# Sparse attention and a two-layer FFN on one core: block-diagonal query tiles, and an order of work taken from a modelled timeline

## Chip, cores, metric

The kernel runs on one core of a Trainium2 chip. The metric is device time in microseconds (us), lower is better. The engines are named as the profile names them: PE is TensorE (PEld its weight loads), ACT ScalarE, DVE VectorE, POOL GpSimd, SP SyncE. Each takes its instructions in the order in which the program put them in its queue.

## What is computed

```python
B, H, S, D = q.shape                      # 8, 8, 576, 64
scores = scale * np.matmul(q, k.transpose(0, 1, 3, 2))
mask_local = (rel >= 0) & (rel < stride)  # stride 32, heads 0 to 3
mask_strided = (rel >= 0) & (pos[None, :] % stride == pos[:, None] % stride)  # heads 4 to 7
...                                       # masked softmax
attn_out = np.matmul(attn, v)
x = attn_out.transpose(0, 2, 1, 3).reshape(B * S, H * D)   # 4608 x 512
r = np.maximum(x @ w_in, 0.0)             # 512 x 2048
out = (s * (r * r) + b) @ w_out           # 2048 x 512
```

## The kernel before

Attention runs batch by batch, four pairs of heads in each: pairs 0 and 1 are local, 2 and 3 strided. A local pair cuts the 576 positions into six blocks of 96 queries with 128 keys; a strided one into eight groups of 72. `pair_steps(b, m)` lists the steps of a pair: transposes of q and k into `ps_t` (L169), copied to `qTl`, `kT_loc`, `qTs`, `kTs` by ScalarE (L180, L185); scores into `ps_s` (L205), one matmul per head and block, on 64 of the 128 rows, since a head has 64 values and a pair of heads (or of groups) lies in the two halves; exp on ScalarE (L211) and a mask product on VectorE (L216) into `pt`; the product with v into `ps_a` (L234), whose last column is the row sum; reciprocal (L240) and division (L242) into `x_nat`; the transposes back (L257) and the copy into `xT` (L263, L265). `load_qk`, `load_v`, `load_w_in` and `load_w_out` are issued by POOL; `pair_heads` has four VectorE copies (L121) that put the two heads of local q and k side by side.

The FFN goes over nine blocks of 512 rows. `ffn_steps(T)` gives 64 matmuls of 512 columns for the first product (`ff1`, L302: 16 groups of four, then relu L307 on ScalarE and the square L308 on VectorE into `gT`) and 64 for the second (`ff2`, L317: four groups of 16, then L322 on VectorE and a store by SP). `emit_bcs` (L340) sums w_out's rows for the bias once.

Of the eight banks of PSUM `ps_t` and `ps_s` have two each, `ps_a` one, `ps_f` three. The order is the program's own (`manual_schedule`). Batch 0 runs alone; then block T of the FFN is emitted with the steps of batch T + 1 spread between its first 112 matmuls at an even distance:

```python
for i, f in enumerate(seq):
    at.setdefault(int(i * 112 / len(seq)), []).append(f)
```

Blocks 7 and 8 have no batch beside them. What ScalarE and VectorE do for a step is emitted with its last matmul, so all queues have the order of the steps.

Of the kernel before, what the change touches and what calls it, by code (L numbers as in the profile page):

```python
# [9 lines left out]
FP16 = mybir.dt.float16  # L10
FP32 = mybir.dt.float32
AF = mybir.ActivationFunctionType
ALU = mybir.AluOpType


@with_exitstack
def kernel(
# [64 lines left out]
    sched = ctx.enter_context(tc.manual_schedule())  # L82

# [11 lines left out]
    for i in range(2):  # L95
        nc.vector.memset(kT_loc[i][:, 0:LPAD], 0.0)

# [50 lines left out]

    def pair_steps(b, m):
# [5 lines left out]
        half = nt // 2  # L155
        nk = 128 if loc else SQ
        st = {}
        T, SS, A0, A1, X = [], [], [], [], []

        def trans(name, j):  # L160
            def f():
                if j == 0:
                    st["p" + name] = psum.tile([128, S], FP16, tag="t", bufs=2, name="ps_t")
                ps = st["p" + name]
# [5 lines left out]
                    out=ps[:, nq * j:nq * j + nq], lhsT=src,  # L170
                    rhs=ident[0:nq, 0:nq], is_transpose=True)
                if j == nt - 1:
                    if loc:
                        if name == "q":
                            st["q"] = qkp.tile([128, S], FP16, tag="qTl", name="qTl")
                            dst = st["q"]
                        else:
                            st["k"] = kT_loc[mm]
                            dst = st["k"][:, LPAD:LPAD + S]
                        nc.scalar.copy(  # L180
                            out=dst.rearrange("d (p j) -> d p j", j=nt),
                            in_=ps.rearrange("d (j p) -> d p j", j=nt))
                    else:
                        st[name] = qkp.tile([128, S], FP16, tag=name + "Ts", name=name + "Ts")
                        nc.scalar.copy(out=st[name], in_=ps)  # L185
            return f

        for name in ("q", "k"):
            for j in range(nt):
                T.append(trans(name, j))  # L190

        def grp(j):

            return (j // half, j % half) if loc else (j % 2, j // 2)

        def score(e, j):
            def f():
                g, i = grp(j)
                if i == 0:
                    st["s", e, g] = psum.tile([128, 3 * LQ], FP32, tag="s", bufs=2, name="ps_s")  # L200
                ps = st["s", e, g]
                c = i * nq
                r0, at = (64 * e, j * nq) if loc else (64 * (j % 2), (4 * e + j // 2) * nq)
                rr = slice(r0, r0 + 64)
                nc.tensor.matmul(  # L205
                    out=ps[0:nk, c:c + nq], lhsT=st["k"][rr, at:at + nk],
                    rhs=st["q"][rr, at:at + nq])
                if i == half - 1:
                    pt = ptp.tile([128, half, nq], FP16, tag="pt" + sfx, name="pt")
                    st["pt", e, g] = pt  # L210
                    nc.scalar.activation(  # L211
                        out=pt[0:nk].rearrange("k t c -> k (t c)"),
                        in_=ps[0:nk, 0:half * nq], func=AF.Exp, scale=scale)
                    mask = (mask_loc if loc else mask_str)[:, None, :].to_broadcast(
                        [nk, half, nq])
                    nc.vector.tensor_tensor(out=pt[0:nk], in0=pt[0:nk], in1=mask, op=ALU.mult)  # L216
            return f

        for a in range(2):
# [185 lines left out]
```

## Time and profile before

| | |
|---|---|
| median of 3 runs (lowest to highest) | 461.65 us (460.33 to 464.23) |
| the profiled execution: time, span | 465.23 us, 463.5 us |
| mean granted TensorE clock | 0.979 |
| busy: PE, DVE, ACT, POOL | 393.1, 198.6, 177.7, 100.1 us |
| matmuls | 2736 |
| HBM read, written | 38.08, 9.44 MB |

A matmul of the profile lasts longer than its slot: matmuls are pipelined, their ends are modelled, and the distance of two starts is what one costs. So busy time says little for TensorE; its timeline and the waits say more. All numbers of the profile belong to the one profiled execution.

### The profile page before, as it was taken

Reading aid. Unit: us, or ns where it says so; the run is one execution under the profiler, and the core shown is the slowest. Engines: PE = TensorE matmul, PEld = TensorE weight load, DVE = VectorE, ACT = ScalarE, POOL = GpSimd, SP = SyncE. Lnnn points to the kernel's source line nnn. Section 1 sums busy time; section 2 is a strip of 40 time slices with the busy share of each in tenths; the row PEclk is TensorE's granted clock in tenths of the full one; section 3 lists DMA queues with packets and bytes.
Section 4 is the critical chain, followed back from the end, with each engine's and each line's share of the span. In section 5 each row is a group of like instructions: output and inputs, shape, how many; then the busy total and the mean of one; then the engine's idle time right before and its main releaser. Section 6 shows DMA issues by size and latency. Waiting matters only on the chain.

```text
span 463.5 us, 6912 instructions
## 1 busy us (share of the span) xinstructions
PE 393.1 (85%) x2736; PEld 194.7 (42%) x2736; DVE 198.6 (43%) x557; ACT 177.7 (38%) x354; POOL 100.1 (22%) x137
## 2 busy tenths in 40 slices
PE   1848799788978989788978898888969797999995
PEld 0633344344434444344434343444434343444442
DVE  1552434444453444434444444434444355352431
ACT  2614651065503751065414651166305541260530
POOL 6736436510244012510252022400000000000000
PEclk9999999899999999899999999899999999899999
DMA  8999999960567114850458025700001001101101
GB/s 108 93 204 100 164 156 141 88 103 1 60 75 87 32 25 60 68 102 0 61 75 119 1 30 67 82 24 1 24 24 45 1 0 47 45 2 46 47 23 69
DMA packets 72516, 28.99 MB, mean 63 GB/s; under 512 B 53028, under 2 KB 67876, under 8 KB 72484
## 3 DMA queue, kind: packets, MB, share of 16 engines
q0 software_dynamic: 66640, 19.04, 44.1%
q1 hardware_dynamic: 5844, 9.51, 5.6%
q8 instruction: 21, 0.34, 0.3%
q14 instruction: 11, 0.09, 0.1%
HBM read 38.08 MB, written 9.44 MB: 103 GB/s over the span
## 4 chain that ended last, share of the span: by engine, by line
PE 71%; DVE 9%; ACT 7%; DMA 6%; issue 3%; POOL 2%; ACTq 0%; POOLq 0%
PE ps_f L302 27%; PE ps_f L317 26%; PE ps_s L205 9%; DVE x_nat L242 5%; PE ps_a L234 4%; ACT u L307 4%; DMA kl<-in_k_dram 3%; PE ps_t L169 3%; DMA qs<-in_q_dram 2%; ACT kT_loc L180 2%; DVE rec L240 2%; PE ps_t L257 1%; DVE o L322 1%; DVE gT L308 1%; ACT kTs L185 1%
## 5 line engine op out<-in xcount | busy, mean ns | idle before, releaser
L302 PE MATMUL ps_f<-xT,w_in_sb 128*128 128x512 f16 x576 | 178.2, 388 | 0.0
L317 PE MATMUL ps_f<-w_out_sb,gT 128*128 128x512 f16 x576 | 166.9, 393 | 0.0
L307 ACT ACTIVATE u<-ps_f 128x512 f16<-128x512 f32 x144 | 86.0, 597 | 72.9 <-PE ps_f L302 72.3
L308 DVE TENSOR_TENSOR gT<-u 128x512 f16<-128x512 f16 x144 | 61.3, 426 | 109.2 <-ACT u L307 109.2
L317 PEld LDWEIGHTS <-gT 128*128 128x128 f16 x576 | 58.0, 102 | 39.1 <-issue 4.3
L234 PEld LDWEIGHTS <-pt 72*72 72x72 f16 (+1 forms) x448 | 44.1, 127 | 71.3 <-DVE x_nat L242 58.3
L211 ACT ACTIVATE pt<-ps_s 72x288 f16<-72x288 f32 (+1 forms) x128 | 48.2, 407 | 59.8 <-PE ps_s L205 58.4
L302 PEld LDWEIGHTS <-w_in_sb 128*128 128x128 f16 x576 | 56.8, 99 | 33.4 <-issue 0.6
L234 PE MATMUL ps_a<-v_str,pt 72*72 72x65 f16 x256 | 39.1, 211 | 29.1 <-DVE x_nat L242 28.8
L265 ACT COPY xT<-ps_t 128x576 f16<-128x576 f16 x16 | 10.2, 639 | 108.6 <-PE ps_t L257 108.6
L242 DVE TENSOR_TENSOR x_nat<-ps_a,rec 72x256 f16<-72x256 f32 (+1 forms) x96 | 44.6, 465 | 3.3
L322 DVE SCALAR_TENSOR_TENSOR o<-ps_f,s_sb,bcs 128x512 f32<-128x512 f32 x36 | 26.9, 747 | 37.1 <-PE ps_f L317 37.1
L134 POOL DMA_DIRECT2D v_str<-in_v_dram x32 | 28.0, 875 | 65.5 <-PE ps_a L234 45.4
L240 DVE RECIPROCAL rec<-ps_a 72x4 f32<-72x4 f32 (+1 forms) x96 | 17.4, 181 | 53.3 <-PE ps_a L234 52.5
L234 PE MATMUL ps_a<-v_loc,pt 128*96 128x65 f16 x192 | 27.3, 209 | 13.2 <-DVE x_nat L242 13.2
L205 PE MATMUL ps_s<-qTl,kT_loc 64*128 64x96 f16 x192 | 26.3, 221 | 11.3 <-ACT kT_loc L180 11.3
L205 PE MATMUL ps_s<-qTs,kTs 64*72 64x72 f16 x256 | 34.4, 222 | 0.8 <-ACT pt L211 0.5
L205 PEld LDWEIGHTS <-kTs 64*72 64x72 f16 x256 | 16.6, 112 | 33.1 <-issue 32.8
L257 PE MATMUL ps_t<-ident,x_nat 72*128 72x72 f16 (+1 forms) x224 | 29.9, 215 | 0.5 <-DVE x_nat L242 0.5
L133 POOL DMA_DIRECT2D v_loc<-in_v_dram x32 | 28.7, 898 | 6.1 <-DVE x_nat L242 2.3
L216 DVE TENSOR_TENSOR pt<-pt,mask_str 72x288 f16<-72x288 f16 x64 | 19.0, 304 | 25.2 <-ACT pt L211 25.1
L205 PEld LDWEIGHTS <-kT_loc 64*128 64x128 f16 x192 | 11.6, 95 | 40.2 <-issue 23.5
(37 smaller groups left out, 251.3 us busy)
## 6 DMA issues: line engine op xcount, KB each, us to landing
out_dram<-o SPq DMA_DIRECT2D x36, 256.0 KB, 2.1
v_loc<-in_v_dram POOLq DMA_DIRECT2D x32, 80.0 KB, 3.5
ql<-in_q_dram POOLq DMA_DIRECT2D x8, 288.0 KB, 5.3
kl<-in_k_dram POOLq DMA_DIRECT2D x8, 288.0 KB, 6.2
qs<-in_q_dram POOLq DMA_DIRECT2D x8, 288.0 KB, 6.6
ks<-in_k_dram POOLq DMA_DIRECT2D x8, 288.0 KB, 8.1
v_str<-in_v_dram POOLq DMA_DIRECT2D x32, 72.0 KB, 3.6
w_in_sb<-in_moe_w_in_dram POOLq DMA_DIRECT2D x4, 512.0 KB, 9.7
```

The lines of the kernel that those rows point to most:

```text
L133: nc.gpsimd.dma_start(out=vl[:, h, 1:LT, 0:D], in_=src)
L134: nc.gpsimd.dma_start(out=vs[:, h, :, 0:D], in_=v[b, 4 + h].rearrange("(p j) d -> p j d", j=ST))
L205: nc.tensor.matmul(out=ps[0:nk, c:c + nq], lhsT=st["k"][rr, at:at + nk], rhs=st["q"][rr, at:at + nq])
L211: nc.scalar.activation(out=pt[0:nk].rearrange("k t c -> k (t c)"), in_=ps[0:nk, 0:half * nq], func=AF.Exp, scale=scale)
L234: nc.tensor.matmul(out=ps[0:nq, j % per, :], lhsT=st["pt", e, grp(j)[0]][0:nk, grp(j)[1], :], rhs=vt[0:nk, 2 * mm + e, j, :])
L242: nc.vector.tensor_tensor(out=st["x"][:, j0:j0 + per, 64 * e:64 * e + 64], in0=ps[0:nq, 0:per, 0:D], in1=rec[0:nq, 0:per].to_broadcast([nq ...
L257: nc.tensor.matmul(out=ps[:, nq * j:nq * j + nq], lhsT=st["x"][:, j, :], rhs=ident[0:nq, 0:nq], is_transpose=True)
L302: nc.tensor.matmul(out=st["h"], lhsT=w_in_sb[:, ct, ft * 128:(ft + 1) * 128], rhs=xT[ct][:, tok0:tok0 + PS], start=(ct == 0), stop=(ct == 3))
L307: nc.scalar.activation(out=u, in_=st["h"], func=AF.Relu)
L308: nc.vector.tensor_tensor(out=st["g"][:, ft, :], in0=u, in1=u, op=ALU.mult)
L317: nc.tensor.matmul(out=st["o"], lhsT=st["g"][:, ft, ts * 128:(ts + 1) * 128], rhs=w_out_sb[:, ft, :], start=(ft == 0), stop=(ft == NFT - 1))
L322: nc.vector.scalar_tensor_tensor(out=o, in0=st["o"], scalar=s_sb[:, 0:1], in1=bcs, op0=ALU.mult, op1=ALU.add)
```

## The change

Three parts:

- A pair's transposed q goes into a tile `qD` in two half copies: head (or group) 0 into columns 0 to nq - 1 of rows 0 to 63, the other into the next nq columns of rows 64 to 127; the rest is zeroed once at the start. One score matmul on all 128 rows then gives both heads (or groups): 28 a batch instead of 56, of 192 or 144 columns. `ps_s` groups hold two (local) or three (strided) of them; exp and mask go over these groups.
- `ps_f` is split: two banks `ps_f1`, one bank `ps_f2`. First and second product each have a list of their own, and the second product of a block can run between groups of the first of the next.
- All steps are emitted by a loop that keeps a modelled time `plan.t`. A step may go when its inputs are done by the model; ScalarE and VectorE work is emitted in the order in which the model has it ready, copies on the engine that would end them earlier. Attention goes first while its share lags behind the FFN's (`due`), and up to three pairs are open. Loads have modelled arrivals: constants at the start, later 12 us (q, k local), 16.5 us (strided) and 16 us (v) after the call, which follows the last k transpose, or the last product with v, of the batch two earlier.

```diff
+class Plan:
...
+    LAT = 70.0
...
+    def flush(self):
+        while True:
+            best = None
+            for p in self.pend:
+                r = self.ready_at(p[0])
+                if r is not None and r <= self.t and (best is None or r < best[0]):
+                    best = (r, p)
+            if best is None:
+                return
+            r, p = best
+            self.pend.remove(p)
+            eng = min(p[1], key=lambda e: max(self.free[e], r) + p[1][e])
+            end = max(self.free[eng], r) + p[1][eng]
+            self.free[eng] = end
+            p[2](eng)
+            for k in p[3]:
+                if isinstance(k, Group):
+                    k = ("rel", k.tag, k.n)
+                self.done[k] = end + self.LAT
...
+    def emit(self, s):
+        if s.group is not None:
+            s.group.n = self.count.get(s.group.tag, 0)
+            self.count[s.group.tag] = s.group.n + 1
+        s.fn()
+        self.t += s.ns
+        for k in s.keys:
+            self.done[k] = self.t + self.LAT + 60
+        for p in s.posts:
+            self.post(*p)
...
+    qD_loc = [const.tile([128, LT, 2, LQ], FP16, name=f"qD_loc{i}") for i in range(2)]
+    qD_str = [const.tile([128, ST, 2, SQ], FP16, name=f"qD_str{i}") for i in range(2)]
...
+        nc.vector.memset(qD_loc[i], 0.0)
+        nc.vector.memset(qD_str[i], 0.0)
...
+    TB, SB, AB, F1B, F2B = 2, 2, 1, 2, 1
+
+    def copy_on(eng, **kw):
+        (nc.scalar.copy if eng == "A" else nc.vector.tensor_copy)(**kw)
...
+                    def half(e):
+                        def g(eng):
+                            hs = slice(64 * e, 64 * e + 64)
+                            ps, qD = st["pq"], st["q"]
+                            if loc:
+                                copy_on(eng,
+                                        out=qD[hs, :, e, :].rearrange("d t (p j) -> d t p j", j=nt),
+                                        in_=ps[hs].rearrange("d (j t p) -> d t p j", j=nt, t=nt))
+                            else:
+                                copy_on(eng, out=qD[hs, :, e, :],
+                                        in_=ps[hs].rearrange("d (j p) -> d j p", j=nt))
+                        return g
+
+                    s.posts = [([key], {"A": 620, "V": 750}, half(e), [("q", e, id_)])
+                               for e in range(2)]
...
-                r0, at = (64 * e, j * nq) if loc else (64 * (j % 2), (4 * e + j // 2) * nq)
-                rr = slice(r0, r0 + 64)
+                if i % per_s == 0:
+                    st["s", g] = psum.tile([128, 3 * 2 * SQ], FP32, tag="s", bufs=SB, name="ps_s")
+                c = i % per_s * 2 * nq
                 nc.tensor.matmul(
-                    out=ps[0:nk, c:c + nq], lhsT=st["k"][rr, at:at + nk],
-                    rhs=st["q"][rr, at:at + nq])
-                if i == half - 1:
-                    pt = ptp.tile([128, half, nq], FP16, tag="pt" + sfx, name="pt")
-                    st["pt", e, g] = pt
+                    out=st["s", g][0:nk, c:c + 2 * nq], lhsT=st["k"][:, i * nq:i * nq + nk],
+                    rhs=st["q"][:, i].rearrange("d e c -> d (e c)"))
...
+                s.posts = [([key], {"A": 170 + 0.83 * 2 * n * nq}, ex, [("e", id_, g), group]),
+                           ([("e", id_, g)], {"V": 150 + 0.52 * 2 * n * nq}, ms,
+                            [("p", id_, g)])]
...
+                s.posts = [([key], {"V": 185}, rc, [("r", id_, e, j)]),
+                           ([("r", id_, e, j)], {"V": 150 + 1.1 * 64 * per}, mu,
+                            [("x", id_, e, j), group])]
...
+            s.posts = [([key], {"A": 600}, rl, [("u", T, ft), group]),
+                       ([("u", T, ft)], {"V": 430}, sq, [("g", T, ft)])]
...
+            s.posts = [([key], {"V": 760}, ev, [group])]
...
+    def fetch(b, at):
+
+        load_qk(b)
+        arrive([("in", "ql0", b), ("in", "kl0", b)], at)
+        arrive([("in", "qs", b), ("in", "ks", b)], at + 4500)
+        plan.post([("in", "ql0", b), ("in", "kl0", b)], {"V": 2000},
+                  lambda eng: pair_heads(b), [("in", "ql", b), ("in", "kl", b)])
+
+    fetch(0, 10000.0)
     load_v(0)
+    arrive([("in", "vl", 0), ("in", "vs", 0)], 22500.0)
     load_w_in()
-    load_qk(1)
+    for c in range(4):
+        arrive([("w_in", c)], 25700.0 + 2700 * c)
+    fetch(1, 38000.0)
     load_v(1)
+    arrive([("in", "vl", 1), ("in", "vs", 1)], 48000.0)
     load_w_out()
-    pair_heads(0)
-    seq, last = batch_steps(0)
-    for f in seq + last:
-        f()
-    pair_heads(1)
+    arrive([("w_out",)], 61000.0)
...
+        if b + 2 < B:
+            def more_qk(b=b):
+                fetch(b + 2, plan.t + 12000.0)
+
+            def more_v(b=b):
+                load_v(b + 2)
+                arrive([("in", "vl", b + 2), ("in", "vs", b + 2)], plan.t + 16000.0)
+            last_t.after = more_qk
+            last_av.after = more_v
...
+        pos = (i1 + i2) / 64.0 + 0.1
+        return (pos if pos <= 1 else 1 + (pos - 1) / 2) * batch_ns
...
+        active = [p for p in range(len(att)) if at_i[p] < len(att[p])][:3]
+        for p in active:
+            r = plan.step_ready(att[p][at_i[p]])
+            if r is not None and r <= plan.t:
+                cand = p
+                break
...
+        order = []
+        if i1 < len(f1):
+            order.append(1)
+        if i2 < len(f2):
+            order.append(2)
+        if len(order) == 2 and i1 % 4 == 0 and i1 > i2 + 64:
+            order.reverse()
+        if i1 % 4:
+            order = [1]
+        for o in order:
+            s = f1[i1] if o == 1 else f2[i2]
+            r = plan.step_ready(s)
+            if r is not None and r <= plan.t:
+                main = o
+                break
+        if cand is not None and (att_done < due() or main is None):
+            s = att[cand][at_i[cand]]
+            plan.emit(s)
+            at_i[cand] += 1
+            att_done += s.ns
+        elif main == 1:
+            plan.emit(f1[i1])
+            i1 += 1
+        elif main == 2:
+            plan.emit(f2[i2])
...
```

## Rows read from the trace of the kernel before

**Rows 1.** The page, part 1: busy us (share of the span) x instructions of each engine.
```profile
PE 393.1 (85%) x2736; PEld 194.7 (42%) x2736; DVE 198.6 (43%) x557; ACT 177.7 (38%) x354; POOL 100.1 (22%) x137
```

**Rows 2.** Chain that ended last, in order of time: start us, length us, what.
```profile
95.67 0.51 issue
...
352.16 0.51 issue
...
403.13 13.81 PE ps_f L302 x64
...
458.42 0.75 DVE o L322
```

**Rows 3.** Timeline of TensorE: start us, us, engine, line, operation, tiles, shapes, count.
```profile
301.09 0.38 PE L302 MATMUL ps_f<-xT,w_in_sb 128*128 128x512 f16 x1
301.31 0.25 PE L169 MATMUL ps_t<-ident,qp 96*128 96x96 f16 x2
301.40 0.38 PE L302 MATMUL ps_f<-xT,w_in_sb 128*128 128x512 f16 x1
...
316.24 0.38 PE L302 MATMUL ps_f<-xT,w_in_sb 128*128 128x512 f16 x1
316.46 0.24 PE L234 MATMUL ps_a<-v_loc,pt 128*96 128x65 f16 x2
316.53 0.38 PE L302 MATMUL ps_f<-xT,w_in_sb 128*128 128x512 f16 x1
```

**Rows 4.** The same timeline where the score matmuls (L205) are interleaved.
```profile
303.58 0.39 PE L302 MATMUL ps_f<-xT,w_in_sb 128*128 128x512 f16 x1
303.90 0.22 PE L205 MATMUL ps_s<-qTl,kT_loc 64*128 64x96 f16 x2
304.05 0.39 PE L302 MATMUL ps_f<-xT,w_in_sb 128*128 128x512 f16 x1
304.37 0.21 PE L205 MATMUL ps_s<-qTl,kT_loc 64*128 64x96 f16 x1
304.52 0.39 PE L302 MATMUL ps_f<-xT,w_in_sb 128*128 128x512 f16 x1
```

**Rows 5.** Waits from 301.62 to 352.16 us: us in total, times, longest.
```profile
PEld L205 <- issue: 7.8, 34, 0.3
...
PE ps_a L234 <- DVE x_nat L242: 5.3, 7, 1.6
...
PE ps_s L205 <- ACT kT_loc L180: 1.4, 2, 0.9
```

**Rows 6.** Timeline of all engines around one wait for x_nat.
```profile
316.99 0.19 PE L234 MATMUL ps_a<-v_loc,pt 128*96 128x65 f16 x1
317.57 0.43 DVE L308 TENSOR_TENSOR gT<-u 128x512 f16<-128x512 f16 x1 [0.70 <-ACT u L307]
...
318.14 0.55 DVE L242 TENSOR_TENSOR x_nat<-ps_a,rec 96x384 f16<-96x384 f32 x1
...
318.75 0.23 PE L234 MATMUL ps_a<-v_loc,pt 128*96 128x65 f16 x1 [1.56 <-DVE x_nat L242]
```

**Rows 7.** Groups of instructions: xcount | busy us, mean ns | idle before.
```profile
L180 ACT COPY qTl<-ps_t 128x576 f16<-128x576 f16 x16 | 10.2, 638 | 17.5 <-PE ps_t L169 17.4
...
L263 DVE COPY xT<-ps_t 128x576 f16<-128x576 f16 x16 | 7.2, 451 | 3.6 <-PE ps_t L257 3.5
```

**Rows 8.** Timeline of POOL: where w_out and the loads of batch 2 are issued.
```profile
45.11 1.18 POOL L145 DMA_DIRECT2D w_out_sb<-in_moe_w_out_dram  x1
...
46.95 0.71 POOL L104 DMA_DIRECT2D kl<-in_k_dram  x1
```

**Rows 9.** The view of tile kl: its eight loads, from issue to landing.
```profile
DMA to landing us min/median/max: 5.7/6.2/17.2
```

**Rows 10.** Timeline of VectorE: the two copies that pair k of batch 1.
```profile
37.38 0.62 DVE L121 COPY kp<-kl 96x768 f16<-96x768 f16 x2 [2.11 <-DMA kl<-in_k_dram]
```

**Rows 11.** Timeline of TensorE in batch 0, where only attention runs.
```profile
29.55 0.45 PE L234 MATMUL ps_a<-v_str,pt 72*72 72x65 f16 x4 [0.72 <-DVE x_nat L242]
```

More of the change, by code (lines that the diff above doesn't have):

```diff
@@ L13, with __init__, ready_at, post @@
 ALU = mybir.AluOpType
+class Plan:
+    LAT = 70.0
+    def __init__(self):
+        self.t = 0.0
+        self.done = {}
+        self.pend = []
+        self.free = {"A": 0.0, "V": 0.0}
+        self.count = {}
+    def ready_at(self, needs):
+        if any(k not in self.done for k in needs):
+            return None
+        return max([self.done[k] for k in needs], default=0.0)
+    def post(self, needs, cost, fn, keys):
+        self.pend.append((needs, cost, fn, keys))
+    def flush(self):
[17 more added lines that the diff above has]
+                self.done[k] = end + self.LAT
+    def step_ready(self, s):
+        r = self.ready_at(s.needs)
+        if r is None:
+            return None
+        if s.group is not None:
+            n = self.count.get(s.group.tag, 0)
+            if n >= s.group.bufs:
+                k = ("rel", s.group.tag, n - s.group.bufs)
+                if k not in self.done:
+                    return None
+                r = max(r, self.done[k])
+        return r
+    def emit(self, s):
+        if s.group is not None:
+            s.group.n = self.count.get(s.group.tag, 0)
[6 more added lines that the diff above has]
+            self.post(*p)
+        if s.after is not None:
+            s.after()
+    def advance(self):
+        nxt = [v for v in self.done.values() if v > self.t]
+        assert nxt, "nothing left that could make a step ready"
+        self.t = min(nxt)
@@ L16, with __init__ @@
+class Group:
+    def __init__(self, tag, bufs):
+        self.tag, self.bufs, self.n = tag, bufs, None
+class Step:
+    def __init__(self, fn, ns, needs=(), group=None, keys=(), posts=(), after=None):
+        self.fn, self.ns, self.needs, self.group = fn, ns, needs, group
+        self.keys, self.posts, self.after = keys, posts, after
 @with_exitstack
@@ L224, in pair_steps, with p_of, av @@
+            return s
+        gr = None
+        for i in range(nt):
+            if i % per_s == 0:
+                gr = Group("s", SB)
+            steps.append(score(i, gr))
+        def p_of(e, j):
+            i, r = (j, e) if loc else (4 * e + j // 2, j % 2)
+            return i // per_s, i % per_s * 2 + r
         per = nt if loc else nt // 2
         vt = (v_loc if loc else v_str)[b % NV]
-        def av(e, j):
+        def av(e, j, group):
             def f():
@@ L253, in f, with xtrans @@
+                s.posts = [([key], {"V": 185}, rc, [("r", id_, e, j)]),
+                           ([("r", id_, e, j)], {"V": 150 + 1.1 * 64 * per}, mu,
+                            [("x", id_, e, j), group])]
+            return s
+        for e in range(2):
+            for j in range(nt):
+                if j % per == 0:
+                    gr = Group("a", AB)
+                steps.append(av(e, j, gr))
+        st["last_av"] = steps[-1]
+        def xtrans(j, group):
             def f():
@@ L342, in emit_bcs, with arrive @@
         nc.scalar.activation(out=bcs, in_=ps, func=AF.Copy, scale=b_sb)
-    load_qk(0)
+    def arrive(keys, at):
+        for k in keys:
+            plan.done[k] = at
+    def fetch(b, at):
[5 more added lines that the diff above has]
+    fetch(0, 10000.0)
@@ L378 @@
+    while plan.pend:
+        plan.flush()
+        if plan.pend:
+            plan.advance()
 _INS = ['q', 'k', 'v', 'moe_w_in', 'moe_w_out', 'moe_s', 'moe_b']
```

295 lines of the change are left out of this document (157 added, 138 removed).

## Prediction, made before the changed kernel ran

> **What bounds the kernel now.** The page's busy shares come first: TensorE 85%, ScalarE and VectorE under half [rows 1]; so TensorE is the engine to look at, and what it stands still for. The chain of waits gives the period. Six times in the middle of the kernel it passes the same point of the loop over blocks, from 95.67 to 352.16 us; that is five periods, (352.16 - 95.67) / 5 = 51.3 us each [rows 2]. The stretch at its end has no attention in it: 64 products take 13.81 us, 215.8 ns each [rows 2]. The 128 products of a block are then worth 128 x 0.2158 = 27.6 us, so seven periods carry 51.3 - 27.6 = 23.7 us each for one batch of attention. The question is what those 23.7 us are.
>
> The timeline of TensorE answers it. Two small matmuls of 96 columns between two large ones stretch the distance of the large ones from 0.216 to 0.31 us, so each costs 0.047; with 65 columns, 0.29 us, so 0.037 [rows 3]. The 56 transposes of q and k, 56 products with v and 28 transposes back of a batch cost 140 x about 0.04 = 5.6 us. The score matmuls, which use 64 rows of the array, behave differently: the distance is 0.47 us, with two of them in it and with one [rows 4]. So 0.47 - 0.216 = 0.25 us is paid per interruption, of which the columns explain about 0.04 to 0.08; the remaining 0.17 to 0.21 us goes into changing between 64 and 128 rows. The table of waits counts 34 of these in one period [rows 5]; 34 x 0.25 = 8.5 us, of which about 6.5 us is changing over.
>
> The rest, 23.7 - 5.6 - 8.5 = 9.6 us, is standing still. The table of waits names two [rows 5]: TensorE waits 7 times for the normalised x_nat (5.3 us), twice for kT_loc (1.4 us). These waits count from the modelled end of the matmul before, 0.38 - 0.216 = 0.16 us after its issue slot, so nine waits are worth 9 x 0.16 = 1.5 us more: 8.2 of the 9.6 us are found. The longest shows why [rows 6]: ps_a has one buffer; the last product before it starts at 316.99, but VectorE first does a square (gT, which itself waited for the relu) and only then the division that frees ps_a, and TensorE starts at 318.75. It is an order problem, not a full engine.
>
> **The change, part by part.**
>
> *Block-diagonal queries.* Per batch 56 score matmuls of 64 rows become 28 of 128 rows: 12 with 192 columns and 16 with 144. 512 columns in 0.2158 us are 2.37 columns per ns, and 96 columns cost 0.047; with 0.004 to spare for each they take 12 x 0.085 + 16 x 0.065 = 2.1 us. That replaces 8.5 us: 6.4 us saved per batch. The Trainium skill speaks against this step: "TensorEngine Tiling (Array Packing)", section Theoretical Speedup, gives products with 64 contraction rows up to twice the rate when they are packed in row tiles. The trace agrees that a packed second score matmul is free (0.47 us with one or two). By that rule alone the step would lose half of the new 2.1 us, 1.1 us a batch; by the rows the interruption outweighs it.
> The price outside TensorE is that a q copy becomes two half copies, each of 64 partitions and still 576 long. On ScalarE one costs what a whole copy costs, 0.638 us [rows 7]. On VectorE no row shows the regrouping copy; the plain one from PSUM takes 0.451 [rows 7], and twice that, 0.9, is my upper bound. I take 0.75, which is nearer to ScalarE's row. Four more copies a batch are 2.6 us, in a period in an engine pair that is busy for 38 and 43% [rows 1]: hidden. If the cover goes, it is 2.6 x 8 = 21 us at most. Zeroing the four qD tiles stands on VectorE before the first load has landed, and costs nothing. The exponentials and masks get fewer and longer, the same elements: nothing.
>
> *Order from the plan, second product beside the first.* Steps are put in TensorE's queue when the plan takes their inputs for ready, and the work of ScalarE and VectorE in the order in which it becomes ready. A square whose relu isn't done no longer stands before a division, and with second-product matmuls as filler there is nearly always something to issue. I expect the 9.6 us per period to fall, not to vanish: the queues stay in order, and the plan gives 0.13 us from the end of a matmul's slot to its reader, where the rows give 0.16 us of pipeline and a start a few hundredths later. With some 36 bank groups a batch and 0.03 to 0.04 us late at each, that is 1.3 us. Bounds: 0 and 9.6.
> Cost at the end: ps_f2 has one bank, and the last three groups of the second product have nothing beside them. Each waits for an eviction of 0.75 us [rows 2] and two hand-overs, about 1.0 us: 3 us.
>
> *The start, which gets worse.* The diff gives every later load a fixed arrival, 12 us after the plan's time of the call. For batch 2 this is wrong. I followed the plan by hand from its own constants, for the order alone: products with v of batch 0 are held until 22.5, the last k transpose of batch 0 comes at about 26.4, so pair_heads(2) counts as ready at 38.4, directly behind pair_heads(1) at 38.0 and ahead of all but the first square of block 0 and all masks of batch 1. On the chip POOL issues these loads only behind w_out, which goes out at 45.11; kl follows at 46.95 [rows 8] behind it. The longest of the eight loads of kl took 17.2 us [rows 9]; I take it for this one, so it lands at 64.15. POOL's order up to there is not changed. VectorE finishes pair_heads(1) at 38.0 [rows 10] and then stands in pair_heads(2) until 64.15 + 0.62 = 64.8 us. Behind it: u has three buffers, so ScalarE stops at the fifth relu, ps_f1 has two banks, so TensorE stops after some six groups. From about 40 to 64.8 nearly nothing moves.
>
> *The sum.* At 64.8 the work still to do before the dense part is 10 groups of first product and batch 1. Its limit is the single ps_a bank: the four products (0.45) and the wait for their division (0.72) took 1.17 us per group [rows 11], and for six I take 1.4. Twelve groups are 8 x 1.17 + 4 x 1.4 = 15.0 us, behind about 6 us of transposes, scores, exponentials and masks: 85.8 us. Then on TensorE 1152 - 64 = 1088 products x 0.2158 = 234.8; the 16 bias products 3.5 and the wait for their copy, as long as that of an eviction, 1.0; six batches x (5.6 + 2.1 = 7.7) = 46.2; six x 1.3 = 7.8 of stalls; 3 at the end; and 463.5 - 458.4 = 5.1 from the last product to the end of the span [rows 2]. 85.8 + 234.8 + 4.5 + 46.2 + 7.8 + 3 + 5.1 = 387.2 us of span. The profiled execution took 465.23 for a span of 463.5, so 389 us; the median of the runs, 461.65, is 0.8% under it: **386 us**. Both ends of the unknowns: stalls 0 gives 378, a slow VectorE copy with no cover adds up to 21.
>
> **Rivals.**
> *A: as above*, 376 to 401.
> *B: the early stall doesn't arise* (pair_heads(2) falls later in VectorE's queue than I put it, or the loads land earlier). For it: my order is worked out by hand. Against it: it needs the plan's ready time to move from 38 to over 60 us. The dense part would begin at about 61 us, where the diff itself puts the landing of w_out, 24.8 us earlier: 386 - 25 = 361.
> *C: the drains go but the standing still stays.* For it: the queues are in order, ps_a still has one bank, and nothing in the trace has run this order. Against it: VectorE and ScalarE are busy for under half, and the waits found are order waits. With 9.6 us left per period instead of 1.3 the time is 386 + 6 x 8.3 = 436; half of it, 411.
> *D: slower than before.* One mechanism: at each of the 36 bank groups of a batch TensorE arrives at the moment the plan names and the operand is late, with nothing allowed past. The waits for x_nat now cost 5.3 / 7 + 0.16 = 0.92 us each. If each group cost that, 36 x 0.92 x 6 = 199 us would come on top. It decides from (462 - 378) / 216 = 0.39 us a group. Against it: scores and products with v have other pairs and FFN steps between them, so their inputs mostly wait for them.
>
> **How the numbers follow.** A 0.58, B 0.14, C 0.20, D 0.08. The likeliest is A, 386 us. The range must hold 0.8: from 361, which keeps most of B, to 420, which holds the lower half of C; outside are D (0.08), the upper part of C (0.08) and the lower edge of B (0.03). A change under about 1% cannot be told from none with this kernel's runs; A, B and C all lie beyond 1% on the fast side. Faster 0.92, within 1% 0.02, slower 0.06.
>
> **What would show it.** In the changed kernel: no wait of the score weights with "issue" as its releaser, and 28 score matmuls a batch; VectorE idle from about 38 to 64 us with the releaser DMA kl at a pairing copy; large products every 0.216 us once attention is done; a mean of under 38 us per batch in the middle. I would be wrong if that idle stretch is missing or shorter than 15 us (B), or if waits for x_nat, pt or copies still sum to over 5 us per batch (C).

## The result, and the profile after

The changed kernel takes **408.0 us** (median of four runs, 406.4 to 409.1) against 461.0 for the kernel before on the same chip: a ratio of 0.884, with a 95% interval of 0.878 to 0.890. The forecast was 386 us: the change is faster as forecast, by 22 us less. The profiled execution took 407.57 us, 405.5 of them span; the sum had given 387.2 us of span.

The page of the changed kernel: part 1 (busy us, share of the span, instructions), and of part 2 the rows of TensorE and of its granted clock, in 40 slices of 10.1 us.

```profile
PE 338.8 (84%) x2512; PEld 187.8 (46%) x2512; DVE 198.0 (49%) x545; ACT 183.9 (45%) x338; POOL 101.5 (25%) x137
...
PE   0665505967999799979997999799899999999884
...
PEclk9999955985999999989999999999999999999999
```

Against [rows 1] TensorE has 224 matmuls fewer and is still busy for the same share. The row in slices says where to look: a 5 and a 0 in the slices from 41 to 61 us, a 6 and a 7 from 81 to 101 us, and from there one weaker digit in every fourth slice, which is once per batch. From 295 us on it is full but for the end. The clock has its 5s in and right behind the two weak stretches, and one 8 in the slice from 172 to 182 us.

The chain of waits: start us, length us, what.

```profile
46.21 17.34 DMA kl<-in_k_dram
...
67.45 1.71 PE ps_f L448 x4
...
97.71 5.51 PE ps_f L506 x16
...
103.98 1.02 PE ps_f L484 x4
...
141.87 0.86 PE ps_f L484 x4
...
180.05 1.42 PE ps_f L484 x4
...
258.08 0.86 PE ps_f L484 x4
...
400.88 0.75 DVE o L495
```

It passes the same point, the first groups of a block, at 141.87 and three periods later at 258.08: 116.21 / 3 = 38.7 us a batch, where [rows 2] gave 51.3. Its last piece, from 400.88, is the copy behind the last product. It also shows the start: a load of `kl` that lasts until 63.6, and then no bias (L506) before 97.7. The sum had put that at 85.8.

The clock is in both of these means. In the changed kernel two of the three periods took 38.2 us; the one from 180.05 to 219.91 took 39.9, and it begins with four large matmuls in 1.42 us instead of 0.86, at a granted clock of 0.50 from 180.5 to 183.5. In the kernel before, three of the five periods took 51.7 to 52.0 us at a mean granted clock of 0.97, and two took 50.5 at 1.00. The second of these two is the period whose waits [rows 5] counts, here in the windows view (the last section names its columns):

```profile
301.62:352.16 50.54, 43.79 (x326) 21.68 (x325) 23.30 (x67) 20.74 (x43) 0.00 (x0) 1.00 0.06 22
```

At the full clock a period thus fell from 50.5 to 38.2 us.

The early stall is where the working by hand had put it. The timeline of VectorE (start us, us, engine, line, operation, tiles, shapes, idle before and its releaser):

```profile
37.91 0.62 DVE L217 COPY kp<-kl 96x768 f16<-96x768 f16 x2
62.10 0.62 DVE L217 COPY qp<-ql 96x768 f16<-96x768 f16 x2 [23.57 <-DMA ql<-in_q_dram]
63.57 0.62 DVE L217 COPY kp<-kl 96x768 f16<-96x768 f16 x2 [0.84 <-DMA kl<-in_k_dram]
64.11 1.56 DVE L467 TENSOR_TENSOR gT<-u 128x512 f16<-128x512 f16 x4
```

The pairing copies of batch 2 stand in VectorE's queue directly behind those of batch 1 [rows 10], and for 23.6 us nothing behind them runs. Three squares stood there ready, one for each buffer of `u`; the fourth relu waited for the first of them, and first products stood behind that.

The table of waits over the whole execution (us in total, times, longest us), with the rows that answer to [rows 5] and one of the stall:

```profile
ACT u L463 <- DVE gT L467: 19.5, 1, 19.5
...
PE ps_a L373 <- DVE x_nat L391: 8.4, 14, 1.3
...
PE ps_t L269 <- ACT qD_loc L248: 7.6, 4, 1.9
...
PEld L324 <- issue: 2.7, 9, 0.5
```

The score weights' wait for "issue", 34 times and 7.8 us in the one period of [rows 5], is down to 9 times and 2.7 us in the whole execution. The wait for `x_nat`, 7 times and 5.3 us a period there, is down to 14 times and 8.4 us in all. The relu's 19.5 us for the squares is the stall as ScalarE saw it. What else is new is a wait of up to 1.9 us for a copy into `qD_loc`.

### The profile page after: what moved, and what is told of

The parts are those of the page before. It is cut to its first block, busy times and chain, and to the rows that moved or that the text cites. A ratio compares the mean times of both kernels' runs of the same rounds, so it can differ in the third digit from the quotient of the medians.

```text
span 405.5 us, 6425 instructions
## 1 busy us (share of the span) xinstructions
PE 338.8 (84%) x2512; PEld 187.8 (46%) x2512; DVE 198.0 (49%) x545; ACT 183.9 (45%) x338; POOL 101.5 (25%) x137
## 4 chain that ended last, share of the span: by engine, by line
PE 73%; DMA 11%; ACT 5%; DVE 5%; POOL 4%; issue 2%; POOLq 0%; ACTq 0%
PE ps_f L484 30%; PE ps_f L448 29%; DMA kl<-in_k_dram 4%; DMA ks<-in_k_dram 4%; PE ps_a L373 4%; PE ps_t L269 3%; PE ps_s L324 3%; DMA qs<-in_q_dram 3%; ACT qD_loc L248 2%; PE ps_t L412 2%; DVE qD_loc L248 2%; DVE x_nat L391 1%; PE ps_f L506 1%; ACT pt L337 1%; DVE o L495 1%
## 5 line engine op out<-in xcount | busy, mean ns | idle before, releaser
L448 PE MATMUL ps_f<-xT,w_in_sb 128*128 128x512 f16 x576 | 165.5, 392 | 20.7 <-ACT u L463 19.0
L484 PE MATMUL ps_f<-w_out_sb,gT 128*128 128x512 f16 x576 | 156.2, 381 | 4.4 <-DVE o L495 3.6
L448 PEld LDWEIGHTS <-w_in_sb 128*128 128x128 f16 x576 | 56.0, 100 | 69.2 <-issue 24.6
L337 ACT ACTIVATE pt<-ps_s 128x384 f16<-128x384 f32 (+2 forms) x96 | 44.3, 488 | 18.3 <-PE ps_s L324 18.1
L373 PE MATMUL ps_a<-v_str,pt 72*72 72x65 f16 x256 | 32.8, 207 | 7.3 <-DVE x_nat L391 7.2
L248 ACT COPY xT<-ps_t 128x576 f16<-128x576 f16 x30 | 19.2, 639 | 38.1 <-PE ps_t L412 37.9
L229 POOL DMA_DIRECT2D v_loc<-in_v_dram x32 | 28.6, 894 | 16.5 <-DMA v_loc<-in_v_dram 8.9
L205 POOL DMA_DIRECT2D qs<-in_q_dram x8 | 5.9, 743 | 97.6 <-PE ps_t L269 97.6
L324 PE MATMUL ps_s<-qD_str,kTs 128*72 128x144 f16 x128 | 23.5, 238 | 1.1 <-ACT kTs L248 0.8
L324 PE MATMUL ps_s<-qD_loc,kT_loc 128*128 128x192 f16 x96 | 18.7, 274 | 5.6 <-ACT kT_loc L248 4.3
L373 PE MATMUL ps_a<-v_loc,pt 128*96 128x65 f16 x192 | 21.3, 213 | 1.2 <-DVE x_nat L391 1.2
L412 PEld LDWEIGHTS <-x_nat 72*128 72x128 f16 (+1 forms) x224 | 16.3, 104 | 11.2 <-DVE x_nat L391 6.8
L224 POOL DMA_DIRECT2D v_loc<-in_v_dram x32 | 17.4, 543 | 14.4 <-DMA w_out_sb<-in_moe_w_out_dram 10.4
```

The lines of the kernel that those rows point to most:

```text
L248: (nc.scalar.copy if eng == "A" else nc.vector.tensor_copy)(**kw)
L324: nc.tensor.matmul(out=st["s", g][0:nk, c:c + 2 * nq], lhsT=st["k"][:, i * nq:i * nq + nk], rhs=st["q"][:, i].rearrange("d e c -> d (e c)"))
L337: nc.scalar.activation(out=pt[0:nk, 0:2 * n].rearrange("k t c -> k (t c)"), in_=st["s", g][0:nk, 0:2 * n * nq], func=AF.Exp, scale=scale)
L373: nc.tensor.matmul(out=st["a"][0:nq, j % per, :], lhsT=st["pt", g][0:nk, i, :], rhs=vt[0:nk, 2 * mm + e, j, :])
L412: nc.tensor.matmul(out=st["px"][:, nq * j:nq * j + nq], lhsT=st["x"][:, j, :], rhs=ident[0:nq, 0:nq], is_transpose=True)
L448: nc.tensor.matmul(out=gts["h"], lhsT=w_in_sb[:, ct, ft * 128:(ft + 1) * 128], rhs=xT[ct][:, tok0:tok0 + PS], start=(ct == 0), stop=(ct == 3))
```

## The experiments

Each was timed in three rounds beside the kernel before on the same chip. Ratios are to the kernel before, with 95% intervals. Runs made on different occasions are compared by their ratios, times 461.65 us.

The theory to begin with: the loss is the early stall, and order and tiles do in the middle what the sum says. The rivals: that some of the loss lies in the middle, in the order or in the tiles, or that what holds the start is not the stall.

**1. The true arrival of batch 2's loads.** The changed kernel, with the landing of these loads told to the plan as it was measured:

```diff
-                fetch(b + 2, plan.t + 12000.0)
+                fetch(b + 2, 64000.0 if b == 0 else plan.t + 12000.0)
...
-                arrive([("in", "vl", b + 2), ("in", "vs", b + 2)], plan.t + 16000.0)
+                arrive([("in", "vl", b + 2), ("in", "vs", b + 2)],
+                       73000.0 if b == 0 else plan.t + 16000.0)
```

> The changed kernel with two constants of the plan set to what the trace shows for batch 2: its q and k at 64 us (12 us after the call before), its v at 73 us. Nothing else differs. Theory (VectorE stands in pair_heads(2) and holds everything): VectorE has no idle stretch of over 5 us between 38 and 62 us, block 0's first product and batch 1 run there, and the dense part begins at about 70 us instead of 104; half a batch of attention that ran before 98 us now runs later (4 us): 375 to 386 us against 408. Rival (the machine waits for the loads anyway, so the stall is only the form the wait takes): less than 8 us gained, 400 to 408.

Measured: 394.3 us, 0.850 [0.845, 0.855]. By the ratios that is (0.884 - 0.850) x 461.65 = 16 us faster than the changed kernel, and a miss all the same. VectorE's stall of 23.6 us is gone. The timelines of VectorE, then of TensorE, in this kernel show what took its place:

```profile
74.34 0.62 DVE L217 COPY qp<-ql 96x768 f16<-96x768 f16 x2 [6.71 <-DMA ql<-in_q_dram]
...
76.89 0.39 PE L373 MATMUL ps_a<-v_str,pt 72*72 72x65 f16 x4 [7.34 <-DVE x_nat L391]
...
80.92 4.50 PE L506 MATMUL ps_f<-w_out_sb,ones 128*128 128x512 f16 x16
```

Batch 3's loads are late in the same way (6.7 us). And the bias, which needs only `w_out` (run 7 starts it at 59.9), still begins at 80.9. Something else holds the dense part back.

**2. The tiles alone.** The kernel before, its own order kept, with nothing of the change but the block-diagonal queries (one half copy on ScalarE, one on VectorE):

```diff
+                        for e, eng in ((0, nc.scalar.copy), (1, nc.vector.tensor_copy)):
...
+                                eng(out=qD[hs, :, e, :].rearrange("d t (p j) -> d t p j", j=nt),
+                                    in_=ps[hs].rearrange("d (j t p) -> d t p j", j=nt, t=nt))
...
+                    out=st["s", g][0:nk, c:c + 2 * nq], lhsT=st["k"][:, i * nq:i * nq + nk],
+                    rhs=st["q"][:, i].rearrange("d e c -> d (e c)"))
```

> The kernel before with the block-diagonal query tiles alone: 28 score matmuls a batch on 128 rows, q copied in two halves, one on ScalarE and one on VectorE; order, banks and loads as before. Theory (34 changes of rows a period cost about 0.19 us each): no wait of the score weights for issue, the period falls from 51.3 by 5 to 7 us, 410 to 425 us against 461. Rival (the changes fill time in which TensorE would wait for the other engines anyway): the waits for x_nat and kT_loc grow by what the scores save, 440 to 461. Rival (two score matmuls in the two halves of the array were nearly free, so wider ones cost more): 461 to 470.

Measured: 408.7 us, 0.884 [0.878, 0.890], the same as the whole change and just under the theory's 410 to 425. The chain passes the same point twice, at

```profile
80.90 1.51 PE ps_f L327 x7
...
341.84 1.51 PE ps_f L327 x7
```

and again six periods later, 43.5 us each. Against 51.3 that is 7.8 us a batch for the tiles, where the sum had 6.4. This kernel's mean granted clock is 1.00, so 0.8 of the 7.8 is clock: against the period of 50.5 us at 1.00 it is 7.0. The table of waits of this kernel over the whole execution shows that the standing still is untouched, some seven waits a batch as in [rows 5]:

```profile
PE ps_a L244 <- DVE x_nat L252: 44.4, 57, 1.4
```

So the two halves of the change can be seen apart. The plan's order takes the period from 43.5 on to 38.7, nearly 5 us a batch, and loses all of that again at the start.

**3. The order alone.** The changed kernel with 64-row score matmuls and whole q copies as before:

```diff
-                    out=st["s", g][0:nk, c:c + 2 * nq], lhsT=st["k"][:, i * nq:i * nq + nk],
-                    rhs=st["q"][:, i].rearrange("d e c -> d (e c)"))
+                    out=ps[0:nk, c:c + nq], lhsT=st["k"][rr, at:at + nk],
+                    rhs=st["q"][rr, at:at + nq])
```

> The changed kernel without block-diagonal tiles: scores on 64 rows as before, one whole q copy, two score groups open at a time; plan, split banks and interleaved products as in the changed kernel. Theory: the plan emits scores in runs, so fewer interruptions a period than 34, perhaps 15 to 25, at about 0.2 us each, less the 1 us of wider columns: 2 to 4 us a period, 422 to 438 us against 408. Rival (the diagonal tiles carry the whole gain): 450 to 462.

Measured: 449.4 us, 0.971 [0.965, 0.976], at the rival's end. Without the tiles the order is worth 3%, and the wait of the score weights is back (table of waits):

```profile
PEld L314 <- issue: 49.5, 186, 0.8
```

What the tiles are worth is thus (0.971 - 0.884) x 461.65 = 40 us here and, in run 2, (1 - 0.884) x 461.65 = 54.

**4. No interleaving of the products.** In the changed kernel, no first product of a block before the second of the block before it is all issued:

```diff
         if i1 % 4:
             order = [1]
+        elif i2 // 64 < i1 // 64:
+            order = [2]
+        else:
+            order = [1]
```

> The changed kernel, but the first product of a block starts only when all 64 matmuls of the second product of the block before are issued, and the other way round. Theory (the second product beside the first gives TensorE something to issue at the evictions of the one ps_f2 bank and while attention is late): three or four evictions of about 1 us a block now stand open where attention doesn't cover them, and each block's change of product waits for relu and square: 2 to 4 us a block, 425 to 445 us. Rival (attention between the matmuls covers them): 404 to 412.

Measured: 390.8 us, 0.843 [0.840, 0.847]. Both expectations fall: taking away the part of the change that was to fill TensorE makes it (0.884 - 0.843) x 461.65 = 19 us *faster*. The chain: the bias starts at 81.9 although the stall is still there, and two batches take 72.0 us.

```profile
81.90 3.47 PE ps_f L506 x16
...
127.98 1.30 PE ps_f L484 x6
...
199.97 1.30 PE ps_f L484 x6
```

So interleaving itself costs something. With that, the timeline of TensorE of the changed kernel was read again, from where this run's bias begins:

```profile
82.31 0.38 PE L448 MATMUL ps_f<-xT,w_in_sb 128*128 128x512 f16 x1
...
82.79 0.38 PE L448 MATMUL ps_f<-xT,w_in_sb 128*128 128x512 f16 x1
...
85.08 0.30 PE L373 MATMUL ps_a<-v_str,pt 72*72 72x65 f16 x4 [0.42 <-DVE x_nat L391]
...
87.30 0.33 PE L373 MATMUL ps_a<-v_str,pt 72*72 72x65 f16 x4 [0.73 <-DVE x_nat L391]
...
89.54 0.63 PE L448 MATMUL ps_f<-xT,w_in_sb 128*128 128x512 f16 x1
...
97.09 0.62 PE L448 MATMUL ps_f<-xT,w_in_sb 128*128 128x512 f16 x1
97.51 5.70 PE L506 MATMUL ps_f<-w_out_sb,ones 128*128 128x512 f16 x16
```

The four single matmuls of L448 are one group: the four column tiles of block 1's first group, each of which waits for the `xT` of its own pair of batch 1. The first came at 82.31, the last at 97.09. Between them the 64 products of block 0's second product, the bias ahead of them, became ready (VectorE ran block 0's last square at 84.16), and not one was issued, while TensorE waited for `x_nat` and for copies. The cause is in two places of the change. A step of the first product asks only for its own `xT`, so the group opens when the batch's first pair is done; and the loop that picks steps holds to an opened group:

```python
        needs = [("xT", bb, ct) for bb in {tok0 // S, (tok0 + PS - 1) // S}]
...
        if i1 % 4:
            order = [1]
```

While a first-product group is open, no second product goes. At the beginning of every block it stays open until the last pair of the batch is through. The second theory follows, the lock: some 15 us are lost at the start (82 to 97.5), and 2 to 3 a period later on. The timeline of TensorE at a later beginning, 214.64 to 219.75, bears this out: four microseconds without a large matmul, then one, and the second product at once behind it.

```profile
214.64 0.81 PE L448 MATMUL ps_f<-xT,w_in_sb 128*128 128x512 f16 x3
...
217.85 0.41 PE L269 MATMUL ps_t<-ident,kp 96*128 96x96 f16 x6 [1.91 <-ACT qD_loc L248]
...
219.53 0.38 PE L448 MATMUL ps_f<-xT,w_in_sb 128*128 128x512 f16 x1
219.75 1.02 PE L484 MATMUL ps_f<-w_out_sb,gT 128*128 128x512 f16 x4
```

**5. The lock alone undone.** The changed kernel, with its interleaving; a group is opened only when all four `xT` of its rows are there:

```diff
-        needs = [("xT", bb, ct) for bb in {tok0 // S, (tok0 + PS - 1) // S}]
+        needs = [("xT", bb, c) for bb in {tok0 // S, (tok0 + PS - 1) // S}
+                 for c in (range(4) if ct == 0 else (ct,))]
```

> The changed kernel, but the first matmul of a first-product group waits in the plan for all four xT tiles of its block, not for its own alone. In the changed kernel a group that is open admits no second-product matmul, and the group that opens a block stands open until the batch's last pair is done. Theory (this lock sets the late start at 97.7 us and the gap of some 3 us in each period): the bias sums begin at about 82 us, as without interleaving (81.9), the period falls from 38.2 to 36 to 36.5 us, clock dips in the middle go away: 382 to 392 us against 408. Rival (the gap comes from ScalarE's queue, where both half copies of q stand behind two exponentials): the period stays over 37.5 us, 395 to 408.

Measured: 385.0 us, 0.833 [0.830, 0.836]. One condition is worth (0.884 - 0.833) x 461.65 = 23.6 us. The chain has the bias at 82.04 and a period of 35.9:

```profile
82.04 3.47 PE ps_f L507 x16
...
234.99 2.59 PE ps_f L485 x12
...
270.93 2.59 PE ps_f L485 x12
```

and VectorE's early stall is untouched (table of waits):

```profile
DVE qp L217 <- DMA ql<-in_q_dram: 24.8, 2, 23.5
```

The lock theory stands. The rest of batch 1's attention, which the changed kernel ran from 82 to 97.5 with only first steps of batch 2 beside it, now lies beside the second product. The granted clock shows no dip in the middle any more.

**6. The rival for the gap of the periods: ScalarE's queue.** The largest wait of the gap above is that for `qD_loc`, 1.9 us, whose copy stands behind exponentials in ScalarE's queue (in the chain the exponentials run from 215.77 us, the two half copies behind them until 217.80). If that order, and not the lock, were what costs, another order of the same queue would cure it. A cheaper price for the pairing copies in the plan moves work about in the queues and leaves the rules of the loop alone:

```diff
-        plan.post([("in", "ql0", b), ("in", "kl0", b)], {"V": 2000},
+        plan.post([("in", "ql0", b), ("in", "kl0", b)], {"V": 1300},
```

> The changed kernel with the plan's cost of pair_heads on VectorE set from 2000 to 1300 ns (1.24 us in the trace), so that one of the two half copies of q may go to VectorE where both stood behind two exponentials on ScalarE. Theory of the lock: what TensorE waits for changes its name, the opened group still admits nothing, the period stays within 1 us of 38.2: 402 to 410 us. Rival (ScalarE's queue order is the cause): the wait of 1.9 us for qD_loc goes and four periods lose 2 us or more, 396 to 402.

Measured: 402.8 us, 0.871 [0.868, 0.874]. The time lies at the border of the two expectations, 402, so the period has to decide. The bias still starts late, the period falls to 37.5 (chain):

```profile
98.23 4.33 PE ps_f L506 x16
...
177.67 0.86 PE ps_f L484 x4
...
215.16 0.86 PE ps_f L484 x4
```

In the periods from 140 to 253 us the wait for `qD_loc` fell to 0.5 us in all, and TensorE now waits for `x_nat` at the transposes back instead (table of waits of that stretch):

```profile
PE ps_t L412 <- DVE x_nat L391: 4.0, 3, 1.3
...
PE ps_t L269 <- ACT qD_loc L248: 0.5, 3, 0.2
```

This order of work is worth 38.7 - 37.5 = 1.2 us a period; another wait takes over while the lock is there. Taking the lock away gives 38.7 - 35.9 = 2.8. Neither run has the clock dip that the 38.7 holds; against the 38.2 us at the full clock the two are worth 0.7 and 2.3. The rival had asked for 2 us or more. In run 5, with the plan's prices as in the changed kernel, TensorE never waits for ScalarE's copy into `qD_loc`: with other work to issue, the wait does not show. So the lock is the larger, and the late start, which this run keeps at 98.2 us, went with the lock.

**7. Both causes undone.** Run 5 with the true arrivals for batches 2 and 3:

```diff
-                fetch(b + 2, plan.t + 12000.0)
+                fetch(b + 2, {0: 64000.0, 1: 77000.0}.get(b, plan.t + 12000.0))
...
+                       73000.0 if b == 0 else plan.t + 16000.0)
```

> The group condition of e6_whole_group, with the plan's arrivals for batches 2 and 3 set to what traces show (q and k of batch 2 at 64 us, its v at 73, q and k of batch 3 at 77 us). Theory: VectorE's stalls at pairing copies and the lock are both gone; second product starts right after w_out lands at about 61 us, and then 246 us of large products less block 0's first, with six batches and some 1 us of stall each, follow: 362 to 372 us. Rival (early on attention is limited by loads and the one ps_a bank, whatever the order): 375 to 385.

Measured: 364.1 us, 0.788 [0.785, 0.790]. The stall is worth (0.833 - 0.788) x 461.65 = 21 us once the lock is gone; it had been worth 16 with the lock (run 1, where batch 3's arrival was also still wrong). A period is 35.9 us as in run 5. In the chain the bias starts at 59.85:

```profile
59.85 3.63 PE ps_f L507 x16
```

TensorE is busy for 91% of the span. The timeline of its end shows what is left there: each of the last four groups of the second product waits 0.84 to 0.94 us for the copy that frees the one bank; the first of them:

```profile
339.25 3.61 PE L485 MATMUL ps_f<-w_out_sb,gT 128*128 128x512 f16 x16 [0.94 <-DVE o L496]
```

**8. And two banks at the end.** Run 7, where the last block's groups 0 and 2 use the banks of the first product, which are free by then:

```diff
+                tag, bufs = (("f1", F1B) if T == NBLK - 1 and ts % 2 == 0 else ("f2", F2B))
+                gts["o", ts] = psum.tile([128, PS], FP32, tag=tag, bufs=bufs, name="ps_" + tag)
```

> As e7_both, and the four last groups of the second product take banks of ps_f1 and ps_f2 in turn, since ps_f1 is free by then. Theory: the waits of 0.84 to 1.08 us before each of the last groups go, 3 to 4 us less than e7_both. Rival (the store behind each eviction sets the end): no difference over 1 us.

Measured: 359.9 us, 0.779 [0.776, 0.781], 4.2 us under run 7 on the same chip. The chain's last piece of TensorE has no gap in it:

```profile
338.55 14.69 PE ps_f L486 x68
```

This is the best kernel of the study, 22% under the kernel before.

**9 and 10. The two ideas of the change, priced in the best kernel.** Run 8 without the block-diagonal tiles (the edit of run 3), and run 8 without the interleaving (the edit of run 4):

> e8_both_tail with scores on 64 rows as before (no block-diagonal tiles), all else equal: what the tiles are worth where nothing else holds TensorE. e3_no_diag had 23 waits for the change of rows a batch, 49.5 us in all. Theory (each change costs TensorE about 0.2 us whether or not something else waits): 6 to 7 us a batch less 1 us of wider columns, 40 to 50 us more than e8_both_tail, 398 to 412 us. Rival (with the lock gone the changes fall into slack): under 25 us more.

> e8_both_tail, but first and second product of neighbouring blocks never interleaved (the condition of e5_no_interleave): what the second product beside the first is worth without the lock. Theory (attention covers the evictions in the middle, nothing covers them in the last blocks; ps_f2 has one bank): the period stays at 36 us, the last four blocks without attention wait about 1 us before each second-product group, 6 to 12 us more, 366 to 372 us. Rival (interleaving also carries the middle): over 375 us.

Measured: 398.3 us, 0.859 [0.853, 0.865] without the tiles; 367.75 us, 0.795 [0.790, 0.800] without the interleaving. By the ratios the tiles are worth 37 us, under the 40 to 50 expected, and the interleaving 7.6. Two rows of the tables of waits say why; the first is of the kernel without tiles, the second of that without interleaving.

```profile
PEld L314 <- issue: 48.4, 193, 0.6
```

```profile
PE ps_f L486 <- DVE o L497: 8.2, 13, 0.8
```

Without tiles a period is 42.2 us instead of 35.9. Without interleaving it is 36.0, hardly longer: attention is filler enough there. What the interleaving buys is mostly the wait at the single `ps_f2` bank at the groups of a second product that have no first product beside them, 8.2 us against 2.1 in the best kernel.

## Why the prediction was right in part, point by point

- **The score matmuls: right.** The sum had 6.4 us a batch. The tiles alone gave 51.3 - 43.5 = 7.8 (run 2), or 50.5 - 43.5 = 7.0 between periods at the full clock, and 42.2 - 35.9 = 6.3 in the best kernel (runs 8 and 9). A score of 192 columns now stretches two large matmuls by about 0.08 us (0.085 taken from [rows 3]). The Trainium skill's page "TensorEngine Tiling (Array Packing)" says under Key Properties that changing the tiling mode drains TensorE, and under Theoretical Speedup that packing 64-row products gives up to twice the rate; here the tiles, which give up the packing and with it the changes of mode, are worth 37 to 54 us in three pairs of kernels. The forecast had weighed the second rule against the rows and taken the rows; that stands.
- **What the period before held.** The sum set the waits of one period against 23.7 us of attention, taken from the mean of five, and found 8.2 of 9.6 us of standing still. The mean holds the slower clock of three periods and that one period does not, so 0.8 of the 1.4 us not found is clock.
- **The price of the half copies: right.** The group of the regrouping copy on VectorE (`qD_loc`) has 756 ns each, the plain one (`qD_str`) 459, where 750 was taken for the first between bounds of 451 and 900; on ScalarE a half copy costs what a whole one did [rows 7]. The view of instruction groups of the changed kernel:

```profile
L248 DVE COPY qD_loc<-ps_t 64x576 f16<-64x576 f16 x12 | 9.1, 756 | 5.7 <-ACT qD_loc L248 3.5 <-PE ps_t L269 2.0
```

- **The early stall: right in place, cause and length.** VectorE was to stand from 38.0 to 64.8; it stood from 38.5 to 64.1, behind the loads that POOL issues after `w_out` [rows 8]. Rival B, that it doesn't arise, is out. Its price was given as 25 us; run 7 against run 5 measures 21.
- **The begin of the dense part: this is the step that failed.** The sum let it wait for ten groups of the first product and all of batch 1's attention, gave these 21 us behind the restart, and so came to 85.8. It began at 97.5, 33 us behind the restart. The restart itself (64.1 against 64.8) and the cycle at the `ps_a` bank (85.08 to 87.30 us, two of 1.11, as the 1.17 of [rows 11]) are as given. What is not: the term took the products and the attention for interleaved. From 64 to 80 us 41 first products went out, the first of them at 0.43 us each (44 were left in block 0, eleven groups and not ten), and 18 of batch 1's 56 products with v. The other 38 were left for 80 to 97.5, where little covered their waits. The twelve groups at the `ps_a` bank, given 15.0 us, ran from 71.8 to 95.2, 23 us. And the dense part need not have waited for them at all. Runs 4 and 5, with the same stall, start the bias at 81.9 and 82.0 and put that rest beside the second product. The sum had the wait without asking what makes it. It is the loop's rule that an opened first-product group lets no second product pass; both lines stand in the diff, and were read as what keeps a group together, and not followed to a group whose inputs come 15 us apart. That is +11.7 us.
- **The bias: 4.5 us given, 6.5 measured** (97.51 to 103.98), +2.0. The same 16 sums take 3.5 to 3.6 us in runs 4, 5 and 7 and 5.5 here; the last section has the clock.
- **Stalls of 1.3 us a batch: the size failed, by the same cause.** A period was to be 27.6 + 7.7 + 1.3 = 36.6 us and was 38.7, or 38.2 at the full clock. There the table of waits has three a period, 2.6 us together (`qD_loc` 1.9, `kT_loc` 0.4, `x_nat` 0.2), and with 0.16 us more for each, as the forecast counts them, they make up the 38.2 - 35.3 = 2.9. With the lock undone a period is 35.9, so 0.6 is left of the 1.3; that this is a few hundredths at each bank group, as the forecast reasoned, is not shown. Rival C put 9.6 or half of that in the periods; 38.7 is 3.4 over 35.3, between the forecast and the lower half of C, and for another reason than C's, which was that the standing still for `x_nat` stays.
- **From the bias to the last product: +5.1 us.** The sum had 234.8 + 46.2 + 7.8 + 3 = 291.8 us; from 103.98 to 400.88 it is 296.9. The end itself was nearly right: four gaps of about 0.8 to 1.1 us, 4.2 in all by run 8, where three of 1.0 were given.
- **The rest.** After the last product 4.6 us against 5.1, -0.5. Then 11.7 + 2.0 + 5.1 - 0.5 = 18.3 us, the whole difference of the spans, 405.5 - 387.2. The other 4 of the 22 us come from outside: the forecast set the median 0.8% under the profiled execution, as it was before, and it was 0.1% over it.
- **Rival D** had each bank group pay for a late operand. It is out: TensorE's wait for `x_nat`, 7 times and 5.3 us in one period [rows 5], is 14 times and 8.4 us in the whole execution.
- **The signs it named.** There are 28 score matmuls a batch, VectorE's idle stretch is there (behind the load of `ql`, then that of `kl`), and large products come every 0.216 us at the end (eight in 1.73 us). The score weights' wait for "issue" is not quite gone: 9 times, 2.7 us. The mean of under 38 us a batch was missed. The sign for C, over 5 us of waits a batch, did not come: 2.6 in the periods of the middle.

The range of 361 to 420 holds the result, which lies above rival A's own 376 to 401, by the room that was left for C. The lock itself stood in no rival.

What stays open: of the difference between the 7.8 us a batch that the tiles are worth in the old order and the 6.3 in the best one, 0.8 is clock; where the other 0.7 lies was not tried apart. And the plan's arrival times of batches 2 and 3 in the best kernel are constants chosen from the landings in the changed kernel and in run 1; nothing shows that other numbers would not be better still.

## What to carry to other kernels

When work is put in order by a model, read its rules for what they forbid, not only for what they allow: follow the one group whose inputs arrive furthest apart, and list what is ready and may not pass it. A ready time that is too early in the model puts a wait for a load at the head of an in-order queue, and all that stands behind it pays; the landing measured in a trace belongs in the plan. And when a change of two parts gives the sum of one, run each part alone: here the tiles alone gave as much as the whole change, and the rest was worth a further 49 us once one condition, three arrival times and the last block's banks were mended.

## What the runs showed of the hardware

The windows view of the changed kernel (stretch, length, busy us and count of PE, PEld, DVE, ACT and POOL, granted TensorE clock, DMA share, GB/s):

```profile
50.00:60.00 10.00, 0.00 (x0) 0.00 (x0) 0.00 (x0) 0.00 (x0) 0.58 (x1) 0.53 1.23 200
64.00:70.00 6.00, 4.73 (x14) 2.02 (x14) 4.78 (x13) 4.16 (x9) 4.45 (x6) 0.50 1.67 92
83.00:88.00 5.00, 1.90 (x23) 1.23 (x22) 3.94 (x13) 2.23 (x5) 2.30 (x4) 1.00 0.81 79
89.00:97.00 8.00, 5.32 (x53) 3.99 (x51) 5.16 (x17) 3.71 (x7) 5.46 (x7) 0.50 0.80 49
```

A stall costs more than its length. During the early stall TensorE did nothing, and the granted clock was 0.53, then 0.50, the level of 1.2 GHz, when it started again at 65.27: four large matmuls took 1.71 us at 67.45, 0.43 each, twice the usual 0.216. The lock did the same a second time. From 83 to 88 us TensorE was not idle, but ran small matmuls with waits between them, busy for 1.90 of 5 us, at a granted clock of 1.00; from 89 to 97 us it was 0.50. The 16 bias sums that followed took 5.5 us instead of 3.6, at 0.50 until 101 us and at 1.00 from 102. Behind one of the later gaps it fell a third time: TensorE was busy for 0.09 us from 176 to 178, and the granted clock was 0.50 from 180.5 to 183.5. The gap at 215.7 to 217.9 us left it at 1.00. In the best kernel, where TensorE is busy throughout the stretch from 90 to 100 us, the granted clock there is 1.00.
